# Attention: head pairs 3 to 5 prepared on the common plan, and two transposes moved to another PSUM ring

## The chip, the cores and the metric

The kernel runs on one core of a Trainium2 chip. The metric is device time in microseconds (us), lower is better; the time before is 658.43 us, the median of 3 runs.

## The reference

Attention with a cluster mask over 2 batches x 8 heads, 768 tokens, head size 64, then two dense blocks. The change touches the attention alone:

```python
q_assign = np.argmax(np.einsum('bhsd,hcd->bhsc', q_n, c_n), axis=-1)   # 16 clusters a head
k_assign = np.argmax(np.einsum('bhsd,hcd->bhsc', k_n, c_n), axis=-1)
mask = q_assign[:, :, :, None] == k_assign[:, :, None, :]
scores = np.where(mask, scale * np.matmul(q, k.transpose(0, 1, 3, 2)), -1000000000.0)
attn = np.exp(scores - np.max(scores, axis=-1, keepdims=True))
attn = attn / (np.sum(attn, axis=-1, keepdims=True) + 1e-09)
attn_out = np.matmul(attn, v)
# x = attn_out as 1536 x 512; then x @ w_in, leaky relu, @ w_out; then top-1 of 8 experts with a skip
```

## The kernel before

Two heads of one batch make a head pair, and there are 8 pairs, numbered 0 to 7. A pair takes 12 steps (six blocks of 128 queries for each of its two heads), so the loop at L689 runs 96 steps and some more to drain. One step puts on TensorE the scores of its block (`sps`, L371), the transposes of the probabilities of three steps before (`tps`, L428), and in every second step four matmul pairs with V (`avps`, L443). VectorE takes the row's maximum (`st`, L374), ACT the exponential with the row's sum (`pr`, L389) and the copies of the transposed probabilities to SBUF (`pt`, L435).

Each engine executes its instructions in the order in which the loop writes them. Nothing reorders them, so the order is set by hand.

While pair p runs, later pairs are prepared in the gaps. The function `plan(d)` lists, for one pair, at which step (counted from the start of the pair before; negative steps lie in the pair before that) each part is issued, and in which place of the step: "a0" after the scores, "d" and "pb" at its end. The parts, in order:

- `raw_pe` and `raw_act`, four times: q and k of the pair (tiles `natq`, `natk`) are transposed on TensorE into `rawps` (L179), and ACT copies that into `raw` (L191). After the fourth copy the load of the next pair's q and k is issued on SP's queue (L342, L99).
- `assign_pe`, `assign_act`, `argmax_pe`: products with the centroids (`asps`, L232), their copy (`sc`, L238), and their transpose (`scps`, L244).
- `argmax_0` to `argmax_3`: VectorE finds the best cluster and its one-hot `oh` (L269). One multiply in between, `eq` (L259), runs on GpSimd.
- `mask_pe` and `mask_dve`: the one-hot is transposed on TensorE (`ohps`, L292), and VectorE turns it into mask values `mk` (L298). `mask_dma` then copies these into the operands of the scores.
- `raw_split`, `exchange`: GpSimd splits `raw` into high and low parts (L208, L209), and DMAs copy them across partitions.

`PREPS` at L330 gives each pair its plan. Pairs 2, 3, 4 and 5 use `plan(5)`, `plan(4)`, `plan(3)` and `plan(2)`, pairs 6 and 7 use `plan(1)`. A larger d means later.

Of GpSimd's queue two more things matter. Every six steps it issues two loads `rb` (L414) of the reciprocals of the row sums. They wait until the row, transposed on TensorE (`rcps`, L406), copied by ACT (`rrow`, L408) and written to DRAM by SP (L704), has landed. And it multiplies the result `xr` by them and splits it (L457 to L467).

PSUM tiles come from rings by tag: "S" has two buffers of two banks for the scores, "T" two for the transposed probabilities, "A" one for `avps`, "M" one for nearly everything of the preparation and for `rcps`. A tile waits until the tile that had its buffer before is read. `raw`, `natq`, `natk` and `xr` have one buffer in SBUF each.

Of the kernel before, what the change touches and what calls it, by code (L numbers as in the profile page):

```python
# [11 lines left out]
BF16 = mybir.dt.bfloat16  # L12
# [13 lines left out]
def kernel(  # L26
# [20 lines left out]
    P = 128  # L47
# [30 lines left out]
    def ps_m(shape, name, dt=F32):  # L78
        return psum.tile(shape, dt, tag="M", name=name, bufs=1)
# [207 lines left out]
                                            op0=ALU.mult, op1=ALU.add)  # L287

    def mask_pe(p):
        ps = ps_m([P, 3, P], "ohps", BF16)  # L290
        for j in range(3):
            nc.tensor.transpose(ps[:, j, :], oh_t[p][:, j].rearrange("p g c -> p (g c)"), identb)  # L292
        ps_prep["mk"] = ps
# [19 lines left out]
    def plan(d):  # L313
        return [
            (d - 8, "pb", raw_pe, 0), (d - 7, "a0", raw_act, 0), (d - 7, "pb", raw_pe, 1),
            (d - 6, "a0", raw_act, 1), (d - 6, "pb", raw_pe, 2), (d - 5, "a0", raw_act, 2), (d - 5, "pb", raw_pe, 3),
            (d - 4, "a0", raw_act, 3), (d - 4, "pb", assign_pe, None),
            (d - 3, "a0", assign_act, None), (d - 3, "pb", argmax_pe, None),
            (d - 2, "d", argmax_0, None), (d - 2, "d", argmax_1, None), (d - 1, "d", argmax_2, None),
            (d, "d", argmax_3, None), (d + 1, "pb", mask_pe, None), (d + 2, "a0" if d == 2 else "d", mask_dve, None),  # L320
            (0, "a0", raw_split, 0), (1, "a0", raw_split, 1), (2, "a0", raw_split, 2), (3, "a0", raw_split, 3),
            (3, "d", exchange, 0), (5, "d", exchange, 1), (max(d + 2, 5), "d", mask_dma, None),
        ]

    PREP = plan(1)
    PREP0 = [(3, "a0", assign_act, None), (3, "pb", argmax_pe, None), (4, "d", argmax_0, None), (4, "d", argmax_1, None),
             (5, "d", argmax_2, None), (6, "d", argmax_3, None)]
    PREP1 = [(1, "pb", assign_pe, None), (2, "a0", assign_act, None), (2, "pb", argmax_pe, None), (3, "pb", argmax_0, None), (4, "pb", argmax_1, None), (5, "d", argmax_2, None), (6, "pb", argmax_3, None), (7, "pb", mask_pe, None), (8, "d", mask_dve, None),
             (8, "d", mask_dma, None)]
    PREPS = {0: PREP0, 1: PREP1, 2: plan(5), 3: plan(4), 4: plan(3), 5: plan(2)}  # L330

    def prep(p, r, slot):
        if p >= NP:
            return
        for rr, sl, f, arg in PREPS.get(p, PREP):
            if rr == r and sl == slot:
# [15 lines left out]
    NSTEP = B * NPAIR * 12  # L352
# [49 lines left out]
    rscr = nc.dram_tensor("recip_scratch", (NSTEP // 6, 6, P), F32, kind="Internal").ap()  # L402

    def recip_rows(g):
        ps = (ps_a if g == NSTEP // 6 - 1 else ps_m)([P, P], "rcps")
        nc.tensor.transpose(ps, rcs[g % 2], ident)  # L406
        row = att.tile([6, P], F32, tag="rrow", name="rrow", bufs=2)
        nc.scalar.activation(out=row, in_=ps[0:6, :], func=AF.Copy)  # L408
        rrow_t[g] = row
# [279 lines left out]
    for s in range(NSTEP + 12 + LAG):  # L689
        p, r = divmod(s, 12)  # L690
# [9 lines left out]
        if 0 < gf <= NSTEP // 6:  # L700
            if rf == 4:
                recip_rows(gf - 1)
            elif rf == 5:
                nc.sync.dma_start(rscr[gf - 1], rrow_t.pop(gf - 1))  # L704
        g, kt = divmod(s - 6 - LAG, 6)
# [876 lines left out]
```

## Time and profile before

| | |
|---|---|
| runs, median (lowest to highest) | 658.43 us (658.21 to 659.04) |
| profiled execution | 658.28 us, span 656.6 us |
| TensorE busy | 633.6 us, 96% |
| VectorE busy | 437.2 us, 67% |
| ACT busy | 420.8 us, 64% |
| GpSimd busy | 165.0 us, 25% |

The page calls the engines PE (TensorE), DVE (VectorE), ACT (ScalarE), POOL (GpSimd) and SP. The span runs from the first to the last instruction; the rest of the execution's time lies around it. Attention takes the first 256 us, the first dense block follows, then the experts. In the text "step" is a step of the attention loop, and step 0 of a pair is its first.

### The profile page before, as it was taken

The page shows a single profiled execution, that of the slowest core. Times are in us where ns is not written, and L with a number is a line of the kernel's source. Part 1 is how long each engine was busy: PE and PEld are TensorE (multiplying, and loading weights), DVE is VectorE, ACT ScalarE, POOL GpSimd, SP SyncE. Part 2 cuts the span into 40 slices and gives each one's busy share as a digit, 9 for nine tenths or more (in the row PEclk, how much of TensorE's full clock was granted, in tenths as well). Part 3 has the DMA queues.
Part 4 walks back from the last instruction along what each step waited for, and adds up shares of the span by engine and source line. Part 5 has one row for each costly group of instructions (what it writes and reads, how often), then busy time and mean ns, then how long its engine had stood idle before and what let it go on. Part 6 is the DMA issues. An engine that isn't in the chain of part 4 may idle for free.

```text
span 656.6 us, 10060 instructions
## 1 busy us (share of the span) xinstructions
PE 633.6 (96%) x3599; PEld 490.4 (75%) x3599; DVE 437.2 (67%) x767; ACT 420.8 (64%) x829; POOL 165.0 (25%) x215
## 2 busy tenths in 40 slices
PE   5999999989999999999999999999999999999995
PEld 3767766667767675788888888888888878688874
DVE  6756676676868663898765435645556548999971
ACT  5798887878888985655444444435654356688860
POOL 4234646463727333400000000000000025004211
PEclk9999999999999999999999999999999999999998
DMA  8765646577675518232104000007135337999930
GB/s 193 195 178 148 185 120 189 137 197 180 179 197 146 170 44 306 70 100 97 31 1 192 1 1 0 1 0 257 58 136 192 138 129 265 366 371 358 373 133 27
DMA packets 63636, 99.53 MB, mean 152 GB/s; under 512 B 27697, under 2 KB 31763, under 8 KB 63200
## 3 DMA queue, kind: packets, MB, share of 16 engines
q1 hardware_dynamic: 60304, 90.62, 44.1%
q0 software_dynamic: 3280, 8.24, 3.8%
q8 instruction: 29, 0.48, 0.3%
q14 instruction: 23, 0.19, 0.1%
HBM read 72.73 MB, written 12.70 MB: 130 GB/s over the span
## 4 chain that ended last, share of the span: by engine, by line
PE 83%; ACT 5%; DVE 5%; DMA 2%; issue 2%; POOL 2%; SPq 0%; POOLq 0%; DVEq 0%; ACTq 0%
PE acc L775 19%; PE ups L669 19%; PE sps L371 8%; PE avps L443 8%; PE hps L1273 7%; PE yps L1304 7%; PE tps L428 6%; ACT pr L389 3%; DVE st L374 1%; ACT pt L435 1%; PE hT L1285 1%; PE rawps L179 1%; PE acc L1165 1%; PE x2T L859 1%; PE asps L232 1%
## 5 line engine op out<-in xcount | busy, mean ns | idle before, releaser
L374 DVE TENSOR_REDUCE st<-sps 128x1 f32<-128x768 f32 x96 | 91.6, 955 | 59.8 <-PE sps L371 59.0
L435 ACT ACTIVATE pt<-tps 128x384 f32<-128x384 f32 x192 | 85.4, 510 | 20.0 <-PE tps L428 19.3
L389 ACT ACTIVATE pr<-sps,st 128x768 f32<-128x768 f32 x96 | 88.2, 919 | 14.3 <-DVE st L374 14.0
L428 PE MATMUL tps<-ident,pr 128*128 128x128 f32 x576 | 78.9, 273 | 0.5 <-ACT pt L435 0.5
L669 PE MATMUL ups<-xh,whii 128*128 128x512 f32 x192 | 74.8, 390 | 0.0
L669 PE MATMUL ups<-xh,wloi 128*128 128x512 f32 x192 | 74.7, 389 | 0.0
L669 PE MATMUL ups<-xl,whii 128*128 128x512 f32 x192 | 74.7, 389 | 0.0
L775 PE MATMUL acc<-whio,gh 128*128 128x512 f32 x183 | 73.1, 399 | 0.2 <-DVE g L759 0.2
L443 PE MATMUL avps<-pt,vnat 128*64 128x384 f32 x384 | 72.1, 498 | 0.0
L428 PEld LDWEIGHTS tps<-ident,pr 128*128 128x128 f32 x576 | 67.9, 140 | 5.5 <-ACT pt L435 1.6
L775 PE MATMUL acc<-whio,gl 128*128 128x512 f32 x183 | 71.4, 390 | 0.0
L775 PE MATMUL acc<-wloo,gh 128*128 128x512 f32 x183 | 71.3, 390 | 0.0
L760 ACT ACTIVATE gh<-g 128x512 fp32r<-128x512 f32 x48 | 30.4, 632 | 44.1 <-DVE g L759 44.1
L758 ACT ACTIVATE lk<-ups 128x512 f32<-128x512 f32 x48 | 28.5, 593 | 37.4 <-PE ups L669 30.9
L759 DVE TENSOR_TENSOR g<-ups,lk 128x512 f32<-128x512 f32 x48 | 33.1, 689 | 28.7 <-ACT lk L758 28.6
L762 DVE TENSOR_TENSOR gl<-g,gh 128x512 fp32r<-128x512 f32 x48 | 33.7, 702 | 25.1 <-ACT gh L760 25.1
L1013 POOL DMA_INDIRECT xe<-x_scratch,eix x1 | 1.2, 1169 | 190.0 <-DVE eix L1012 190.0
L646 DVE TENSOR_TENSOR wloi<-rawb,whii 128x512 fp32r<-128x512 f32 x36 | 24.7, 687 | 27.5 <-ACT whii L645 27.4
L443 PEld LDWEIGHTS avps<-pt,vnat 128*64 128x64 f32 x384 | 23.4, 136 | 25.3 <-issue 24.5
L669 PEld LDWEIGHTS ups<-xh,whii 128*128 128x128 f32 x192 | 36.0, 188 | 8.0 <-issue 0.6
L669 PEld LDWEIGHTS ups<-xh,wloi 128*128 128x128 f32 x192 | 36.1, 188 | 7.5
L669 PEld LDWEIGHTS ups<-xl,whii 128*128 128x128 f32 x192 | 36.0, 188 | 7.5
(303 smaller groups left out, 1353.4 us busy)
## 6 DMA issues: line engine op xcount, KB each, us to landing
rawb<-in_moe_w_dram SPq DMA_DIRECT2D x25, 1024.0 KB
rawa<-in_moe_w_dram SPq DMA_DIRECT2D x10, 1024.0 KB
stg<-in_moe_w_in_dram SPq DMA_DIRECT2D x16, 512.0 KB
stg<-in_moe_w_out_dram SPq DMA_DIRECT2D x16, 512.0 KB
UB<-UA SPq DMA_DIRECT2D x16, 192.0 KB
vnat<-in_v_dram SPq DMA_DIRECT2D x8, 384.0 KB
rb<-recip_scratch POOLq DMA_DIRECT2D x32, 96.0 KB, 2.8
w_f_scratch<-cvt SPq DMA_DIRECT2D x12, 256.0 KB
```

Of the source, the lines that this page charges most:

```text
L371: nc.tensor.matmul(ps[:, kh, 0:HS], lhsT=t[0:n, 0, qs], rhs=t[0:n, 1, kh * HS:(kh + 1) * HS], start=first, stop=not first)
L374: nc.vector.tensor_reduce(out=st[:, 0:1], in_=ps[:, :, 0:HS], axis=AX.XY, op=ALU.max, negate=True)
L389: nc.scalar.activation(out=pr, in_=ps[:, :, 0:HS], func=AF.Exp, bias=st[:, 0:1], accum_out=sm_t[g][:, 3 * h + j:3 * h + j + 1])
L428: nc.tensor.transpose(ps[:, t, :], pr[:, kh, t * P:(t + 1) * P], ident)
L435: nc.scalar.activation(out=pt[:, 3 * kh:3 * kh + 3, j, :], in_=t_t[s][kh], func=AF.Copy)
L443: nc.tensor.matmul(av_t[g][64 * h:64 * h + 64, :], lhsT=vnat[p][:, h, kt, :], rhs=pt_t[p, half, h][:, kt].rearrange("p j c -> p (j c)"), s ...
L669: nc.tensor.matmul(ps, lhsT=w[:, cc, :], rhs=x[:, blk, cc, :], start=(n == 0), stop=(n == 3 * KD - 1))
L759: nc.vector.tensor_tensor(out=g, in0=ps, in1=t, op=ALU.max)
L762: nc.vector.tensor_tensor(out=gl, in0=g, in1=_f(gh), op=ALU.subtract)
L775: nc.tensor.matmul(ps, lhsT=a[:, ts_], rhs=w, start=(fc == 0 and n == 0), stop=(fc == NFC - 1 and n == 2))
L1273: nc.tensor.matmul(ps, lhsT=x[:, c, :], rhs=w, start=(n == 0), stop=(n == len(mm) - 1))
L1304: nc.tensor.matmul(ps[:, cs], lhsT=x[:, f, :], rhs=w[:, cs], start=(h == 0 and f == 0 and n == 0), stop=(h == 1 and f == 3 and n == 2))
```

## The change

Pairs 3 to 5 get `plan(1)`, as pairs 6 and 7 have it; pair 2 keeps `plan(5)`. In `plan(d)` the place of `mask_dve` changes for d = 5 alone among the plans that are still used: it goes from step 7 to step 6, right behind `mask_pe`. Pair 2's transposed mask lies in the "T" ring and no longer in "M". The last `rcps` lies in "T" and no longer in "A".

```diff
     def mask_pe(p):
-        ps = ps_m([P, 3, P], "ohps", BF16)
+        ps = (ps_t if p == 2 else ps_m)([P, 3, P], "ohps", BF16)
...
-            (d, "d", argmax_3, None), (d + 1, "pb", mask_pe, None), (d + 2, "a0" if d == 2 else "d", mask_dve, None),
+            (d, "d", argmax_3, None), (d + 1, "pb", mask_pe, None), (d + (d < 5) + 1, "d" if d < 5 else "pb", mask_dve, None),
...
-    PREPS = {0: PREP0, 1: PREP1, 2: plan(5), 3: plan(4), 4: plan(3), 5: plan(2)}
+    PREPS = {0: PREP0, 1: PREP1, 2: plan(5)}
...
     def recip_rows(g):
-        ps = (ps_a if g == NSTEP // 6 - 1 else ps_m)([P, P], "rcps")
+        ps = (ps_t if g == NSTEP // 6 - 1 else ps_m)([P, P], "rcps")
```

On GpSimd, where pair 4 ends and pair 5 begins, the multiply `eq` (L259) of pair 5 stood behind the first split and the two `rb` loads. Before:

```order
L467 TENSOR_TENSOR xl<-xr,xh 128x256
L208 TENSOR_SCALAR UA<-raw 128x384
L209 TENSOR_TENSOR VA<-raw,UA 128x384
L414 DMA rb<-recip_scratch 64x384 x2
L259 TENSOR_TENSOR eq<-eq,cw 128x384
L208 TENSOR_SCALAR UA<-raw 128x384
```

And now:

```order
L467 TENSOR_TENSOR xl<-xr,xh 128x256
L259 TENSOR_TENSOR eq<-eq,cw 128x384
L208 TENSOR_SCALAR UA<-raw 128x384
L209 TENSOR_TENSOR VA<-raw,UA 128x384
L414 DMA rb<-recip_scratch 64x384 x2
L208 TENSOR_SCALAR UA<-raw 128x384
```

The multiply has moved ahead of both; it does the same for pairs 3 and 4.

On TensorE, in steps 6 to 8 of pair 1, behind the transposes of pair 2's mask (`ohps`), the `raw` transposes of pair 3 come in (one more group of them stands a step further up):

```order
 L292 MATMUL ohps<-identb,oh 128x128
-L371 MATMUL sps<-UB 128x384 x2
-L371 MATMUL sps<-VB 128x384 x2
-L428 MATMUL tps<-ident,pr 128x128 x6
+L179 MATMUL rawps<-ident,natq 128x128 x3
+L371 MATMUL sps<-UB 128x384 x2
+L371 MATMUL sps<-VB 128x384 x2
+L428 MATMUL tps<-ident,pr 128x128 x6
+L179 MATMUL rawps<-ident,natk 128x128 x3
```

Two groups of three transposes have come between the mask and the next steps' work.

On VectorE, in steps 6 and 7 of pair 1, the mask's reader (`mk`) of pair 2 stood behind the next maximum and the reciprocal. Before:

```order
L397 TENSOR_SCALAR sm<-sm 128x6
L374 TENSOR_REDUCE st<-sps 128x1
L400 RECIPROCAL rc_114<-sm 128x6
L298 TENSOR_SCALAR mk<-ohps,msc 128x384
L374 TENSOR_REDUCE st<-sps 128x1
```

And now:

```order
L397 TENSOR_SCALAR sm<-sm 128x6
L298 TENSOR_SCALAR mk<-ohps,msc 128x384
L374 TENSOR_REDUCE st<-sps 128x1
L400 RECIPROCAL rc_114<-sm 128x6
L374 TENSOR_REDUCE st<-sps 128x1
```

It stands one maximum earlier.

## Rows read from the trace of the kernel before

**Rows 1.** The page, parts 1 and 2: busy us; tenths in 40 slices.

```profile
PE 633.6 (96%) x3599; PEld 490.4 (75%) x3599; DVE 437.2 (67%) x767; ACT 420.8 (64%) x829; POOL 165.0 (25%) x215
...
PE   5999999989999999999999999999999999999995
```

**Rows 2.** Windows, pairs 1 to 5: stretch, width, busy us by engine, clock, DMA.

```profile
40.66:71.07 30.41, 29.99 (x203) 21.37 (x201) 20.49 (x34) 25.89 (x62) 16.14 (x21) 1.00 0.63 167
71.07:102.65 31.58, 30.64 (x207) 21.27 (x206) 21.17 (x34) 26.76 (x64) 15.67 (x21) 1.00 0.61 165
102.65:133.48 30.83, 29.90 (x203) 21.36 (x200) 20.52 (x33) 24.93 (x60) 17.16 (x21) 1.00 0.65 158
133.48:165.12 31.64, 29.45 (x199) 21.07 (x198) 21.65 (x34) 25.11 (x61) 14.80 (x19) 1.00 0.70 182
165.12:194.43 29.31, 29.31 (x200) 20.98 (x198) 22.31 (x34) 25.63 (x61) 16.43 (x21) 1.00 0.67 189
```

**Rows 3.** Waits of TensorE, 60 to 262 us: total, times, longest.

```profile
PE ohps L292 <- DVE oh L269: 1.7, 2, 1.1
PE rcps L406 <- DVE mk L298: 1.1, 1, 1.1
```

**Rows 4.** Timeline, pair 4: start, us, engine, what, [idle before, releaser].

```profile
137.89 1.11 POOL L414 DMA_DIRECT2D rb<-recip_scratch  x2 [5.19 <-DMA recip_scratch<-rrow]
...
139.01 1.02 POOL L259 TENSOR_TENSOR eq<-eq,cw 128x384 f32<-128x384 f32 x1
...
142.64 0.86 DVE L269 TENSOR_TENSOR oh<-eq,mx 128x384 bf16<-128x384 f32 x1
...
143.56 0.34 PE L292 MATMUL ohps<-identb,oh 128*128 128x128 bf16 x3 [1.12 <-DVE oh L269]
...
145.57 0.67 DVE L298 TENSOR_SCALAR mk<-ohps,msc 128x384 fp32r<-128x384 bf16 x1
...
146.38 0.30 PE L406 MATMUL rcps<-ident,rc 128*128 128x128 f32 x1 [1.07 <-DVE mk L298]
```

**Rows 5.** Timeline, pair 5, where pair 6 is prepared on plan(1).

```profile
166.85 1.01 POOL L259 TENSOR_TENSOR eq<-eq,cw 128x384 f32<-128x384 f32 x1 [4.10 <-DVE eq L256]
...
169.59 1.11 POOL L414 DMA_DIRECT2D rb<-recip_scratch  x2
...
172.46 0.34 PE L292 MATMUL ohps<-identb,oh 128*128 128x128 bf16 x3
...
178.91 1.00 POOL L209 TENSOR_TENSOR VB<-raw,UA 128x384 fp32r<-128x384 f32 x1
...
180.32 0.51 ACT L191 ACTIVATE raw<-rawps 128x384 f32<-128x384 f32 x1
```

**Rows 6.** Windows, steps 5 to 11 of pair 1 and of pair 5.

```profile
54.33:71.07 16.74, 16.41 (x113) 12.33 (x111) 11.99 (x20) 13.66 (x33) 7.30 (x10) 1.00 0.58 154
177.35:194.43 17.08, 17.08 (x121) 12.64 (x119) 11.33 (x17) 14.72 (x37) 6.37 (x10) 1.00 0.69 198
```

**Rows 7.** Timeline, pair 1, steps 6 and 7, around pair 2's mask.

```profile
58.68 0.34 PE L292 MATMUL ohps<-identb,oh 128*128 128x128 bf16 x3
...
59.61 0.82 PE L428 MATMUL tps<-ident,pr 128*128 128x128 f32 x6
59.94 0.17 DVE L397 TENSOR_SCALAR sm<-sm 128x6 f32<-128x6 f32 x1
```

**Rows 8.** Timeline, the end of attention.

```profile
254.55 0.49 ACT L451 ACTIVATE xr<-avps 128x384 f32<-128x384 f32 x1 [1.04 <-PE avps L443]
255.09 0.33 PE L406 MATMUL rcps<-ident,rc 128*128 128x128 f32 x1 [0.68 <-ACT xr L451]
...
260.20 0.49 ACT L451 ACTIVATE xr<-avps 128x384 f32<-128x384 f32 x1 [2.91 <-POOL xl L467]
```

**Rows 9.** DMA view, 42 to 48 us and 48 to 54 us: packets by size.

```profile
DMA packets 3330, 1.26 MB, mean 211 GB/s; under 512 B 3164, under 2 KB 3223, under 8 KB 3329
...
DMA packets 299, 0.89 MB, mean 148 GB/s; under 512 B 53, under 2 KB 53, under 8 KB 299
```

## The prediction

> **What bounds the kernel now.** I read the page first: TensorE is busy for 633.6 of 656.6 us, and in nine tenths and more of nearly every slice [rows 1]. The change touches the attention loop alone (8 head pairs of 12 steps, start to about 256 us) and adds and removes no instruction, so the question is where TensorE stands idle in that loop. The next view is one window per head pair, from the pair's first score matmul to the next pair's [rows 2]. Pair 5's window and pair 4's hold the same kinds and numbers of TensorE work (4 `raw` transposes of three, one `asps`, one `scps`, one `ohps`), yet pair 4 takes 31.64 us and pair 5 takes 29.31 us; the granted clock is 1.00 in both. Pairs 2 and 3 take 31.58 and 30.83 us. TensorE's idle time in the windows (width less busy) is 0.94, 0.93 and 2.19 us in pairs 2, 3 and 4, and nothing in pair 5.
>
> The list of waits says for what [rows 3]: the mask's transpose waits for VectorE's one-hot (1.7 us, twice), the reciprocals' transpose once for the mask's reader (1.1 us). The timeline of pair 4 shows the chain [rows 4]. GpSimd's queue is in order: `eq` of pair 5 stands behind the two `rb` loads, and these wait for the reciprocals' row to land in DRAM, until 137.89. So `eq` starts at 139.01, the one-hot ends at 143.50, TensorE has waited 1.12 us for it, and the mask's reader ends at 146.24, which holds the one "M" bank that the reciprocals' transpose needs: another 1.07 us. In pair 5 the pair being prepared is pair 6, which already has the plan that the change gives to pairs 3 to 5 [rows 5]: `eq` runs at 166.85, ahead of the `rb` loads at 169.59, and the mask's transpose at 172.46 waits for nothing.
>
> **The change part by part.** Each sum is made against the profiled execution (658.28 us, span 656.6); the median of the runs shown is 658.43, 0.15 us more, which I add at the end.
>
> *Pairs 3 to 5 prepared on plan(1).* Every instruction of their preparation moves 3, 2 and 1 steps earlier; the total of work stays. Pairs 2, 3 and 4 get exactly pair 5's content, so I price each by pair 5's window: 31.58 + 30.83 + 31.64 = 94.05 us becomes 3 x 29.31 = 87.93: **-6.12 us**. That includes the work that leaves pair 2 for pair 1 (pair 3's `asps` and `scps`).
>
> *Pair 1 gets fuller.* It keeps pair 2's last preparation and now holds all of pair 3's `raw`, `asps` and `scps`. From its sixth step on it has what pair 5 has there, plus pair 2's mask transposes. The two stretches take 16.74 us in pair 1 and 17.08 us in pair 5 [rows 6]; the three mask transposes are 0.34 us [rows 7]. So 17.42 - 16.74 = +0.68. ACT is late in this stretch: pair 2's `eq` still stands late on GpSimd, and the exponentials wait for VectorE. I allow between 0 and 0.4 us for `asps` waiting on ACT's last `raw` copy, and take **+0.8 us** in all.
>
> *Pair 3's load of q and k.* It is not moved, but its first reader goes from the ninth to the sixth step of pair 1, at 54.33. Between 42 and 48 us 3164 packets under 512 bytes ran, between 48 and 54 only 53 [rows 9]. The two loads make 2 x 1536 such packets (128 x 12 rows of 256 bytes each), so they had landed by about 48, 6 us ahead. Cost nothing; if the 6 us were gone, each us of lateness would be one us of TensorE.
> The Trainium skill (DMA: Bandwidth & Descriptors, Specifications) says that transfers under 512 B miss the line rate. That speaks against a reader that comes sooner; the rows show the load done in time all the same, and by them the sum stays.
>
> *Loads on SP's queue.* The q and k loads of pairs 4 to 6 go ahead of `vnat`, of a weight stage and of the reciprocals' row. This is the order that pair 4 already has for pair 7's load, and pair 5 behind it shows no wait for it. Between nothing and 0.4 us a pair; I take nothing.
>
> *Pair 2's mask in the "T" ring, its reader one step earlier.* The ring has two buffers, and the probabilities' second transpose of the next step now needs the mask's reader done. In pair 1 the mask's transposes run at 58.68 and that transpose follows from 59.61 on, while VectorE comes free for the reader at 60.11 (end of `sm`, 59.94 + 0.17) [rows 7]; with 0.67 us for the reader [rows 4] it ends at 60.78. Left alone that would hold TensorE for about 0.7 us, but two groups of three `raw` transposes stand ahead of it now; estimated at the mask group's 0.34 us each, they push TensorE back by 0.6 to 0.7. So 0.1 us, between 0 and 0.7; it lies in the +0.8.
>
> *Last reciprocals' transpose in the "T" ring.* It waits 0.68 us for ACT's `xr`, because both use the single "A" bank [rows 8]; the probabilities' last copies were done before `xr` began. The wait goes. What is late next: ACT's next `xr` at 260.20 waits for GpSimd, not for TensorE, so the chain behind it does not move fully along. Between 0 and 0.68; I take **-0.5 us**, nearer to the row.
>
> Sum: -6.12 + 0.8 - 0.5 = **-5.8 us**: 658.28 - 5.8 = 652.5, and with the 0.15 us 652.6 us. After attention TensorE's slices are full [rows 1], so what follows starts that much earlier and ends so.
>
> The Trainium skill (Perfetto Trace Analysis, Tensor Engine Instruction (MATMUL, LD_WEIGHTS)) warns that a matmul's reported end is computed, not observed. By this rule the idle time above misses part of the waiting, and start-to-start windows are the better measure; by idle time alone pairs 2 to 4 would give back 4.06 us and not 6.12. The rows bear it out for pair 4: it lost 2.33 us against pair 5 and shows 2.19 idle.
>
> **The rivals.**
> 1. *Only the visible idle returns.* TensorE's work is unchanged, so it can give back no more than it stood idle: 0.94 + 0.93 + 2.19 = 4.06 us, less the 0.4 us that I allowed for ACT in pair 1, and little at the end. For: the work of pair 3 that leaves pair 2 must be done in pair 1. Against: pair 2 loses 2.27 us to pair 5 with 0.94 idle, and its extra `asps` and `scps` need not be the whole rest. 658.43 - 3.7 = 654.7.
> 2. *The change does not do what it says.* Pairs 2 to 4 are slow because of what else runs there (weight stages, q and k loads), not because of the plan. Then the windows keep their widths, pair 1 pays 0.8 and the end returns 0.5: 658.7, no change. For: those loads are there. Against: the chain in rows 4 names GpSimd's order.
> 3. *Slower: the single `raw` buffer.* On plan(1) ACT's first `raw` copy of a pair overwrites what GpSimd's last split of the pair before still reads. In pair 5 that split ends at 179.91 and the copy starts at 180.32: 0.41 us of room [rows 5]. If GpSimd runs later than that in pairs 2 to 4 (its `rb` loads wait for the row's landing, and more q and k packets stand ahead of that row now), ACT blocks, and behind it the copies of the probabilities that TensorE waits for. Each us over 0.41 costs one us in three pairs. It eats the 5.8 us where GpSimd comes 0.41 + 5.8 / 3 = 2.3 us later than in pair 5; at 3 us it is 3 x 2.6 - 5.8 = +2.0: 660.4. Against: in pair 4, where the row lands just before 137.89, the `rb` loads go at 4.4 us into the pair, as in pair 5 (4.5).
>
> **How the numbers follow.** The forecast has 0.66, its own range 651.6 to 654.0 (all of -6.5 to -4.4). Rival 1 has 0.21, rival 2 has 0.07, rival 3 has 0.06. A measurement of this kernel tells 0.2% (1.3 us) from no change; so faster 0.87, same 0.07, slower 0.06. The range that holds 8 in 10 takes the forecast's and most of rival 1's: 651.5 to 656.2.
>
> **What would show it.** In the profile of the changed kernel the windows of pairs 2, 3 and 4 should be 29.0 to 29.6 us wide and pair 1 about 31.2; no wait of the mask's transpose for the one-hot longer than 0.2 us in pairs 2 to 4; `eq` of pairs 3 to 5 in the last step of the pair before, ahead of the `rb` loads; the last reciprocals' transpose without a wait for `xr`. A window of pair 1 above 32, or ACT's `raw` copy waiting for GpSimd, would make the forecast wrong, and so would windows of pairs 2 to 4 that stay above 30.5.

## The result and the profile after

The changed kernel takes 651.87 us, the median of 6 runs (650.17 to 654.0), against 658.4 us of the kernel before. The ratio is 0.9894 with an interval of 0.9873 to 0.9914, a gain of 5.7 to 8.4 us. The forecast of 652.6 us lies inside that interval, but the ratio's own value, 651.4 us (658.4 x 0.9894), lies 0.1 us under the low end of the range. The profiled execution took 651.22 us with a span of 649.3, 7.27 us less than the span before.

The page, parts 1 and 2, answers to [rows 1]:

```profile
PE 631.6 (97%) x3599; PEld 489.9 (75%) x3599; DVE 441.4 (68%) x767; ACT 420.8 (65%) x829; POOL 165.9 (26%) x215
...
PE   5999999999999999999999999999999999999994
```

TensorE does the same 3599 recorded matmuls, is booked as busy for 2.0 us less, and fills 97% of a shorter span. The windows of pairs 1 to 5 and, last, of pair 7 (columns as in [rows 2]; pair 7 has no successor, and its window runs to 0.52 us behind the start of the second group of probability transposes after the loop's last scores):

```profile
40.46:71.42 30.96, 30.87 (x213) 21.77 (x212) 20.71 (x34) 26.35 (x64) 13.96 (x19) 1.00 0.68 167
71.42:100.70 29.28, 29.28 (x199) 20.96 (x198) 22.57 (x34) 25.60 (x61) 16.46 (x21) 1.00 0.66 173
100.70:129.98 29.28, 29.28 (x199) 20.96 (x198) 22.54 (x34) 25.58 (x61) 16.47 (x21) 1.00 0.60 161
129.98:159.09 29.11, 29.11 (x199) 21.00 (x198) 22.50 (x34) 25.55 (x61) 16.13 (x21) 1.00 0.74 196
159.09:188.49 29.40, 29.26 (x199) 21.00 (x198) 21.60 (x34) 25.46 (x61) 16.52 (x21) 1.00 0.68 185
...
215.51:242.92 27.41, 27.16 (x175) 19.66 (x175) 16.91 (x25) 24.08 (x57) 8.72 (x14) 1.00 0.29 103
```

Pairs 2, 3 and 4 lost 2.30, 1.55 and 2.53 us against [rows 2], together 6.38, and TensorE no longer stands idle in them. Pair 1 grew by 0.55.

TensorE's waits in the same stretch as [rows 3], 60 to 262 us; this one row is the whole list:

```profile
PE tps L428 <- ACT pt L435: 0.5, 2, 0.3
```

The waits for the one-hot and for the mask's reader are gone; what is left stands at the drain of attention, where it was before too. [rows 3] shows two of the seven rows that this list had before. The others include 0.9 us of the scores for the exponential (three times) and 0.3 us of the mask's transpose for ACT's `rrow`. In pair 3 TensorE's waits were of these two kinds (0.48 and 0.34 us); none of the two for the one-hot lay there. The timeline of pair 4, rows that answer to [rows 4]:

```profile
131.71 1.01 POOL L259 TENSOR_TENSOR eq<-eq,cw 128x384 f32<-128x384 f32 x1 [4.10 <-DVE eq L256]
...
135.04 1.10 POOL L414 DMA_DIRECT2D rb<-recip_scratch  x2 [0.55 <-DMA recip_scratch<-rrow]
135.27 0.52 DVE L269 TENSOR_TENSOR oh<-eq,mx 128x384 bf16<-128x384 f32 x1
...
137.32 0.34 PE L292 MATMUL ohps<-identb,oh 128*128 128x128 bf16 x3
...
139.60 0.66 DVE L298 TENSOR_SCALAR mk<-ohps,msc 128x384 fp32r<-128x384 bf16 x1
...
140.35 0.30 PE L406 MATMUL rcps<-ident,rc 128*128 128x128 f32 x1
```

`eq` runs 3.3 us ahead of the `rb` loads, and the mask's transpose stands 1.53 us behind the end of the one-hot instead of waiting for it. The reciprocals' transpose follows the end of the mask's reader at 140.26 without a wait on TensorE.

The timeline of pair 5, rows that answer to [rows 5]:

```profile
165.43 1.12 POOL L414 DMA_DIRECT2D rb<-recip_scratch  x2 [1.82 <-DMA recip_scratch<-rrow]
...
173.91 1.31 POOL L209 TENSOR_TENSOR VB<-raw,UA 128x384 fp32r<-128x384 f32 x1
175.26 0.49 ACT L191 ACTIVATE raw<-rawps 128x384 f32<-128x384 f32 x1 [1.15 <-POOL VB L209]
```

Here the row landed later than before: the `rb` loads go 6.3 us into the pair, not 4.5, the last split ends late, and ACT's first `raw` copy waits 1.15 us for it. That is rival 3's mechanism, in one pair; the pair is 0.09 us longer for it.

The timeline of pair 1, steps 6 and 7, answers to [rows 7]:

```profile
58.81 0.34 PE L292 MATMUL ohps<-identb,oh 128*128 128x128 bf16 x3
58.99 0.50 PE L179 MATMUL rawps<-ident,natq 128*128 128x128 f32 x3
...
59.69 0.67 DVE L298 TENSOR_SCALAR mk<-ohps,msc 128x384 fp32r<-128x384 bf16 x1
60.02 0.95 PE L428 MATMUL tps<-ident,pr 128*128 128x128 f32 x6
```

The mask's reader ends at 60.36, while the six transposes of the probabilities run, and none of them waits in the list of waits. The end of attention answers to [rows 8]:

```profile
248.13 0.33 PE L406 MATMUL rcps<-ident,rc 128*128 128x128 f32 x1
248.34 0.49 ACT L451 ACTIVATE xr<-avps 128x384 f32<-128x384 f32 x1 [1.05 <-PE avps L443]
...
253.92 0.49 ACT L451 ACTIVATE xr<-avps 128x384 f32<-128x384 f32 x1 [3.38 <-POOL xl L467]
...
261.41 0.40 PE L775 MATMUL acc<-whio,gh 128*128 128x512 f32 x1
```

The last reciprocals' transpose now stands ahead of `xr`. The last row is the fourth matmul of the first dense block's output, without a wait. Before, it was the row

```profile
268.65 0.50 PE L775 MATMUL acc<-whio,gh 128*128 128x512 f32 x1 [0.16 <-DVE g L759]
```

From the last probability transposes' start to the reciprocals' transpose took 3.04 us before (252.05 to 255.09) and takes 2.30 now (245.83 to 248.13): 0.74 less. From the first to the fourth output matmul took 1.00 us before (267.65 to 268.65) and takes 0.69 now, and up to the tenth 0.41 us are gained. Nothing that follows in the dense blocks is spaced otherwise (0.07 us in 386).

### The profile page after: what moved, and what is told of

Read it like the earlier page. It is cut to its first block, busy times and chain, and to the rows that moved or that the text cites. A ratio compares the mean times of both kernels' runs of the same rounds, so it can differ in the third digit from the quotient of the medians.

```text
span 649.3 us, 10059 instructions
## 1 busy us (share of the span) xinstructions
PE 631.6 (97%) x3599; PEld 489.9 (75%) x3599; DVE 441.4 (68%) x767; ACT 420.8 (65%) x829; POOL 165.9 (26%) x215
## 4 chain that ended last, share of the span: by engine, by line
PE 92%; ACT 2%; POOL 2%; DVE 1%; DMA 1%; issue 1%; SPq 0%; POOLq 0%
PE ups L669 20%; PE acc L775 19%; PE sps L371 10%; PE avps L443 10%; PE tps L428 8%; PE hps L1273 7%; PE yps L1304 7%; PE rawps L179 1%; PE hT L1285 1%; PE acc L1165 1%; PE x2T L859 1%; ACT pr L389 1%; PE asps L232 1%; DMA recip_scratch<-rrow 1%; PE scps L244 1%; PE xT L1034 1%
```

## The experiments

Times in brackets after a median are the lowest and highest run; each ratio is to the kernel before, run on the same chip. The theory behind them: TensorE waited in pairs 2 to 4 because GpSimd's `eq` stood behind the `rb` loads ("G"). The rival: because VectorE's search fell in steps in which VectorE also converts weights ("V").

**The change again (after_again).** No edit.

> The changed kernel once more, unaltered, for a second profile and more rounds. By the theory that the gain lies in pairs 2 to 4, the windows of pairs 2, 3 and 4 are again 29.1 to 29.3 us, pair 1 about 31.0, and the time 650 to 654 us. If the gain outside pairs 1 to 4 (0.5 us in pair 7, 0.4 us in the first dense block) was chance of one execution, these two differ by a few tenths here.

651.85 us (651.7 to 652.4), ratio 0.9895, 0.9877 to 0.9914. Pairs 1 to 5 take 31.44, 29.27, 29.28, 28.99 and 29.95 us. So the gain repeats. Pair 7 takes 27.47 us and the end is as short as in the first profile, so neither was the chance of that one execution. Pair 5 again has ACT's `raw` copy behind GpSimd, 1.69 us this time, and TensorE waits 0.57 for it.

**The last transpose alone (rcps_only).** Kernel before, with

```diff
-        ps = (ps_a if g == NSTEP // 6 - 1 else ps_m)([P, P], "rcps")
+        ps = (ps_t if g == NSTEP // 6 - 1 else ps_m)([P, P], "rcps")
```

> The kernel before with the last reciprocals' transpose in T and nothing else. Theory: the wait of 0.68 us for xr goes and TensorE starts the first dense block 0.68 us earlier; of VectorE's later chain 0 to 0.4 us more. 657.3 to 657.8 us. Rival (the chain behind xr and GpSimd decides): the wait moves to the first dense block's second output product, and the time is within 0.2 us of before.

658.14 us (657.39 to 659.03), ratio 0.9985, 0.9973 to 0.9996. The median lies above the expected 657.3 to 657.8, on a chip where the kernel before took 658.81. In its profile the stretch at the last transposes is 0.74 us shorter than before and the one at the output matmuls, up to the tenth, 0.41; from the drain to the end of the program it gains 1.07 us. (The profiled span is as long as before, 656.6 us, because other stretches took longer in this execution, the start and pairs 1, 2 and 7.) So the trace gives this edit of one ring 1.07 us, the runs 0.3 to 1.8, and the wait for VectorE's `g` went with it: the second gain at the end belongs to this edit too. In the sixteen profiles of this case the reciprocals' transpose comes 2.30 us behind the last transposes wherever it lies in "T", and 3.04 to 3.05 wherever it lies in "A".

**The plans alone (plan1_mask_m).** The changed kernel with both rings put back: pair 2's mask in "M", the last `rcps` in "A".

> The change with pair 2's mask left in the M ring (its reader still at step 6) and the last reciprocals' transpose left in A. Theory: pairs 2 to 4 are 29.1 to 29.3 us as in the changed kernel; in pair 1 the second group of raw transposes waits for the mask's reader, 0.7 to 1.5 us, so pair 1 is 31.7 to 32.5; the wait of 0.7 us for xr at the end is back. In all 652.5 to 654.5 us. Rival (the T ring carries a good part of the gain): pairs 2 to 4 are above 30 us or pair 1 above 33, and the time is above 655 us.

654.56 us (654.26 to 655.65), ratio 0.994, 0.9925 to 0.9955. TensorE's waits from 50 to 270 us:

```profile
PE rawps L179 <- DVE mk L298: 1.3, 1, 1.3
PE rcps L406 <- ACT xr L451: 0.7, 1, 0.7
...
PE acc L775 <- DVE g L759: 0.3, 1, 0.3
```

Pair 1 takes 32.33 us, 0.9 to 1.4 more than with the mask in "T" (30.96 to 31.47 in five profiles): the next `raw` transposes want the "M" bank that the mask's reader holds. Pairs 2 to 4 keep 29.27, 29.28 and 29.00. So the plans bring the pairs' gain, and the rings keep pair 1 and the end from giving back some 2.7 us (of the medians).

**GpSimd's part taken out (eq_vector).** Kernel before, `eq` of pairs 3 to 5 on VectorE.

```diff
-        eng = nc.vector if p == 0 else nc.gpsimd
+        eng = nc.vector if p in (0, 3, 4, 5) else nc.gpsimd
```

> The kernel before with its plans of 5, 4, 3 and 2 steps, but the multiply eq of pairs 3, 4 and 5 on VectorE and no longer on GpSimd. Theory (eq behind the rb loads on GpSimd is the cause): the waits of the mask's transpose for the one-hot go, pairs 2 and 3 come to about 30.2 and 29.6 us (their own extra asps and scps stay), pair 4 to 29.3 to 30: some 3.5 to 4.5 us less than before, 654 to 655 us, without moving any preparation. Rival (the late plans themselves, by the M bank or by weight stages beside them): pairs 2 to 4 stay within 0.5 us of 31.6, 30.8 and 31.6, 658 us; VectorE's extra 0.56 us a pair costs nothing or a little.

659.06 us (658.28 to 661.74), ratio 1.001, 0.9998 to 1.0021: no gain, and G as the only cause falls. Its timeline in pair 3:

```profile
109.44 0.59 DVE L259 TENSOR_TENSOR eq<-eq,cw 128x384 f32<-128x384 f32 x1
109.71 1.19 POOL L209 TENSOR_TENSOR VB<-raw,UA 128x384 fp32r<-128x384 f32 x1
109.95 1.50 DVE L580 SCALAR_TENSOR_TENSOR cvt<-stg,cvt 128x512 uint32<-128x512 uint32 x1
...
111.37 0.95 DVE L374 TENSOR_REDUCE st<-sps 128x1 f32<-128x768 f32 x1
...
112.41 0.90 ACT L389 ACTIVATE pr<-sps,st 128x768 f32<-128x768 f32 x1 [2.74 <-DVE st L374]
...
113.45 0.44 PE L371 MATMUL sps<-UA 80*128 80x384 f32 x1 [1.65 <-ACT pr L389]
```

Here the wait has another name: the search and a weight conversion, this one drawn out beside GpSimd's split, stand ahead of the row's maximum in one step, so the exponential is 2.74 us late and TensorE's scores 1.65. In pair 4 the waits keep their names: 0.63 us for the one-hot (1.12 before) and the same 1.07 for the mask's reader.

**VectorE's part taken out (argmax_r3).** Kernel before with the search of pairs 3 to 5 moved to steps 3 to 6, where its first part meets no conversion; `eq` stays on GpSimd, the transposes of `raw` stay late, masks and the last `rcps` in "T".

```diff
+        v = 5 if d > 1 else 1
...
-            (d - 2, "d", argmax_0, None), (d - 2, "d", argmax_1, None), (d - 1, "d", argmax_2, None),
+            (v - 2, "d", argmax_0, None), (v - 2, "d", argmax_1, None), (v - 1, "d", argmax_2, None),
```

> The kernel before with the plans of 4, 3 and 2 steps for pairs 3, 4, 5, but VectorE's cluster search of these pairs at steps 3 to 6 as pair 2 has it (their masks in T, reader at step 6, the last reciprocals' transpose in T). Everything else of the preparation stays where it was. Steps 3, 7 and 11 hold no weight conversion on VectorE. Theory V (the search costs time where it shares a step with the conversions on VectorE): pairs 2, 3 and 4 fall to about 30.5, 30.0 and 29.7 us, 4 us less in all, and with 0.9 at the end 653.5 to 654.5 us. Theory G (eq has to stand ahead of the rb loads on GpSimd, which it does not here): pairs 2 to 4 stay above 30.8 on average and the time is 656.5 to 658 us.

658.49 us (657.68 to 659.48), ratio 0.9997, 0.9987 to 1.0006. V alone falls too. TensorE's waits from 60 to 160 us, and VectorE's wait for `eq` in pair 3:

```profile
PE tps L429 <- DVE mk L298: 1.9, 3, 0.8
PE ohps L292 <- ACT pt L436: 1.9, 2, 1.2
```

```profile
118.37 0.55 DVE L264 TENSOR_REDUCE mx<-eq 128x24 f32<-128x384 f32 x1 [3.19 <-POOL eq L259]
```

Pairs 2 to 4 take 31.70, 31.65 and 30.31 us, 0.39 less than before in all. At its new place `eq` still stands late on GpSimd, now behind the splits that the `rb` loads hold up, and VectorE waits 3.19 us for it in pair 3 and 2.70 in pair 4. Two parts of this edit have a price of their own: the end gains some 0.8 us from the last `rcps` in "T", and pair 1 is 0.94 us longer, 0.75 of it a wait for pair 2's mask in "T", which has no `raw` transposes behind it here.

**Both, by another way (r3_eq_vector).** The two edits above together; nothing is on `plan(1)`.

> Pairs 3 to 5 keep plan(4), plan(3), plan(2) for their transposes on TensorE, but VectorE's search stands at steps 3 to 6 (first part in step 3, which has no weight conversion) and the multiply eq is done by VectorE, so it passes GpSimd's rb loads altogether. The two halves of the theory are both met, by other means than plan(1). Theory 'both are needed and together they are enough': the waits of the mask's transpose in pairs 2 to 4 go, these pairs take 29.3 to 30.6 us, and the whole about 654 us (653 to 655.5). Rival 'the earlier raw and centroid work on TensorE and ACT is what counts': the pairs stay at 30.3 to 31.7 as with the search alone, and the whole at 658 to 659.

654.74 us (654.25 to 655.45), ratio 0.9938, 0.9917 to 0.996. Pairs 2 to 4 take 30.58, 30.51 and 29.94 us, and of their waits in [rows 3] nothing is left. The whole list from 60 to 165 us, of which the first row lies in pair 1:

```profile
PE tps L429 <- DVE mk L298: 0.8, 1, 0.8
PE rcps L407 <- DVE eq L256: 0.5, 2, 0.3
```

Each edit alone brought nothing, the two together 2.6 to 5.5 us, of which about 1 us is the last `rcps`, as in rcps_only. So two conditions go together: `eq` not late on GpSimd, and the first part of the search not beside a conversion. `plan(1)` meets both. One thing these runs do not separate: in eq_vector VectorE does the 0.59 us of `eq` itself, and no run has `eq` ahead of the `rb` loads on GpSimd with the search left where it was.

`plan(1)` is 2.9 us better still. In pairs 2 to 4 it gives back 6.38 us, these two edits 3.02. The three pairs hold 89.99 us of TensorE work here, as before, and 87.67 in the changed kernel; 1.27 us of that is one pair's `asps` and `scps`, which the change moves into pair 1. The other 2.1 us of the pairs' gain the two conditions do not explain, and no run takes them apart.

**The change without its order on GpSimd (eq_behind).** The changed kernel with `eq` of pairs 3 to 5 issued one step later, behind the `rb` loads (`argmax_1b` is that multiply alone).

```diff
-            (d - 2, "d", argmax_0, None), (d - 2, "d", argmax_1, None), (d - 1, "d", argmax_2, None),
+            (d - 2, "d", argmax_0, None), (d - 2, "d", argmax_1, None), (d - 1, "d", lambda q: argmax_1b(q) if 3 <= q <= 5 else None, None), (d - 1, "d", argmax_2, None),
```

> The changed kernel with one move: eq of pairs 3, 4 and 5 stands on GpSimd behind the rb loads (step 0) and no longer ahead of them; VectorE's compare stays in step 11. Theory G: VectorE stands in its queue until eq is done, some 2 us into each pair, so pairs 2, 3 and 4 become 1.5 to 3 us longer each, 31 to 32 us, and the time 656.5 to 660 us. Theory V: the search is still in a free step, the wait is covered by the two score buffers, pairs 2 to 4 stay below 29.8 us and the time is 652 to 653.5 us.

664.33 us (662.59 to 666.34), ratio 1.0077, 1.0057 to 1.0096. Pairs 2 to 4 take 32.65, 32.32 and 36.89 us. Waits of TensorE, 60 to 165 us, and then windows of 4 us in pair 4 (columns as in [rows 2]); L274 is the one-hot here:

```profile
PE ohps L297 <- DVE oh L274: 6.6, 3, 3.7
PE sps L376 <- ACT pr L394: 4.5, 3, 1.6
```

```profile
146.00:150.00 4.00, 1.37 (x11) 1.34 (x12) 4.00 (x8) 1.75 (x4) 3.27 (x4) 1.00 0.55 125
150.00:154.00 4.00, 2.68 (x11) 2.18 (x10) 3.23 (x5) 3.05 (x8) 1.51 (x2) 0.50 0.56 162
154.00:158.00 4.00, 4.00 (x18) 2.17 (x17) 1.38 (x2) 2.43 (x6) 2.66 (x4) 0.65 0.41 113
158.00:162.00 4.00, 4.00 (x29) 2.83 (x27) 3.61 (x6) 3.31 (x8) 0.19 (x1) 1.00 0.92 198
```

With the order on GpSimd undone the change costs 5 us instead of bringing 7, more than was expected. It is a harder case than the kernel before: there VectorE's next part of the search stands a step behind `eq`, here in the same step. In pair 4 the wait was 3.70 us long, and behind it the granted clock fell to 0.50, the lower level of 1.2 GHz, which makes this pair dearer than the other two; these had waits up to 1.63 us, and their clock stayed at 1.00.

**One pair alone (pair5_only).** Kernel before, pair 5 alone on `plan(1)`.

```diff
-    PREPS = {0: PREP0, 1: PREP1, 2: plan(5), 3: plan(4), 4: plan(3), 5: plan(2)}
+    PREPS = {0: PREP0, 1: PREP1, 2: plan(5), 3: plan(4), 4: plan(3)}
```

> The kernel before with pair 5 alone on plan(1); pairs 2 to 4 keep plan(5), plan(4), plan(3), the last reciprocals stay in A. Pair 5 is prepared while pair 4 runs. Theory 'each pair pays for its own successor's plan': pair 4 goes from 31.64 to 29.0 to 29.5 us, pair 3 (which takes over pair 5's earlier work) stays within 0.6 of 30.83, pairs 1 and 2 stay at 30.4 and 31.6; the whole 656 to 656.8. Rival 'the pairs disturb each other, the gain comes only when all are on the one plan': pair 4 stays above 30.3 or pair 3 loses what pair 4 gains; the whole 658 to 659. On pair 7, which went from 27.88 to 27.41 with the change: it goes with pair 5's plan if it is 27.3 to 27.6 here, and not if 27.8 or more.

657.69 us (656.57 to 659.53), ratio 0.9985, 0.9973 to 0.9997. The whole lies between the two forecasts. Pair 4 comes to 29.29 us, as expected, but pair 3 goes to 32.05, against the expectation. Pair 7 takes 27.96, so its gain does not come with pair 5's plan. The timeline of pair 3:

```profile
116.04 0.33 PE L292 MATMUL ohps<-identb,oh 128*128 128x128 bf16 x3 [0.34 <-ACT rrow L408]
...
118.36 0.67 DVE L298 TENSOR_SCALAR mk<-ohps,msc 128x384 fp32r<-128x384 bf16 x1
...
119.13 0.52 PE L179 MATMUL rawps<-ident,natq 128*128 128x128 f32 x3 [1.36 <-issue]
```

The profile names no releaser, but the transposes start 0.10 us behind the end of the mask's reader (119.03), and both tiles lie in the one "M" bank. Two plans side by side put pair 4's mask and pair 5's `raw` in the same steps; with one plan they lie apart. So here one pair's gain was taken back by its neighbour on another plan. The change avoids this at pair 2, which keeps `plan(5)`, by putting its mask into another ring.

**Rival 3 made to happen (gp_delay).** The changed kernel; GpSimd does the high part of the fourth split of pairs 3, 4 and 5 three, five and seven times over. There is one execution.

```diff
+        for _ in range(2 * (p - 2) + 1 if i == 3 and p in (3, 4, 5) else 1):
+            nc.gpsimd.tensor_scalar(out=hi, in0=raw[:, i, :], scalar1=1.0, scalar2=1.0, op0=ALU.mult, op1=ALU.mult)
```

> The changed kernel with GpSimd's last high-part split of pairs 3, 4 and 5 done 3, 5 and 7 times instead of once (the same values; about 1.0, 2.0 and 3.1 us more), to try the single raw buffer that rival 3 spoke of. By that rival, with about 0.4 us of room, pair 2 becomes 0.6 us, pair 3 1.6 us and pair 4 2.7 us longer than 29.3, 656 us in all, with ACT's raw copy waiting for GpSimd. If the probabilities' copies cover it, the pairs stay within 0.3 us of 29.3 up to 2 us of delay.

659.63 us. The last split ends 15.61, 17.69 and 21.04 us into pairs 2, 3 and 4 (14.37, 14.36 and 14.57 in the changed kernel). ACT's `raw` copies in these pairs:

```profile
87.25 0.49 ACT L191 ACTIVATE raw<-rawps 128x384 f32<-128x384 f32 x1 [0.33 <-POOL VB L210]
...
118.63 0.49 ACT L191 ACTIVATE raw<-rawps 128x384 f32<-128x384 f32 x1 [2.59 <-POOL VB L210]
...
152.95 0.49 ACT L191 ACTIVATE raw<-rawps 128x384 f32<-128x384 f32 x1 [6.05 <-POOL VB L210]
```

Pairs 2, 3 and 4 take 29.29, 30.97 and 35.87 us. A split 1.24 us later costs nothing, one 3.33 us later costs 1.69, and one 6.47 us later 6.76, the last with the granted clock at 0.59 and 0.56 in the two windows of 4 us from 150 to 158 us. TensorE waited 4.9 us until 153.49, so there the clock fell before the wait was over. The chain that rival 3 describes is real; its room is about 1.6 us (3.33 less 1.69) and not 0.41.

**Pair 2 on the common plan too (pair2_plan1, pair2_plan1_a).** The first drops `plan(5)` from `PREPS` and puts pair 1's mask, not pair 2's, in "T", with its reader at step 7 instead of 8. The second puts that mask back in "M" and spreads pair 2's `raw` transposes over "M" and "A":

```diff
-        ps = ((ps_t, ps_t, ps_m, ps_a)[i] if p == 0 else ((ps_t, ps_t, ps_a, ps_t)[i] if p == 1 else ps_m))([P, 3, P], "rawps")
+        ps = ((ps_t, ps_t, ps_m, ps_a)[i] if p == 0 else ((ps_t, ps_t, ps_a, ps_t)[i] if p == 1 else (ps_m, ps_a, ps_a, ps_m)[i] if p == 2 else ps_m))([P, 3, P], "rawps")
```

> The changed kernel with pair 2 on the common plan too: all pairs from 2 on. Its preparation then falls into steps 5 to 11 of pair 0; pair 1's mask goes through T with its reader at step 7. By both theories pair 1 becomes like pair 2, 29.3 us (1.7 to 2.1 less than now), and pair 0 gets three raw transposes, asps and scps more, 0.31 + 0.95 + 0.3 = 1.6 us of TensorE, part of it in its idle 1.3 us: 650.5 to 651.5 us. If ACT cannot take pair 0's copies in time, pair 0 grows by over 2 us and the time is 652 or more.

> The version with pair 2 on plan(1) too, with pair 2's raw transposes spread over the rings A and M (M, A, A, M) and pair 1's mask back in M. There pair 0 took 24.39 us against 23.17 with pair 2 on plan(5), and TensorE waited in it for ACT's raw copies (0.34 and 0.21) and for a probability copy (0.49). Theory 'the one bank M is what makes pair 0 wait': these waits go, pair 0 takes 23.2 to 23.7, the other pairs stay at 29.0 to 29.4, the whole 651.0 to 652.0, level with the changed kernel or 0.5 us faster. Rival 'ACT has no room in pair 0': the waits move to other tiles, pair 0 stays at 24.2 or more, the whole 652.5 to 653.5.

The first took 652.92 us (651.52 to 653.0), ratio 0.9908, 0.9892 to 0.9923: pair 1 fell to 29.37 as expected, but pair 0 rose to 24.39, and it is no better than the change. The second took 650.35 us (650.28 to 652.35), ratio 0.9873, 0.9853 to 0.9892. Its pair 0 takes 23.49, inside the expected 23.2 to 23.7, but not for the expected reason: 0.64 of the 0.90 lie in the very first step, where the first version waited 0.91 us for a DMA and the second did not. From step 6 on, pair 0 takes 13.81 and 13.54, so the rings were worth 0.3 us. In p2a_stg, below, which has the same rings, the wait in the first step is back, and pair 0 takes 24.46. TensorE's waits for ACT in pair 0 moved, as the rival had it. In the second version, 16 to 60 us:

```profile
PE rawps L179 <- ACT raw L191: 0.5, 1, 0.5
PE asps L232 <- ACT raw L191: 0.4, 1, 0.4
```

The two medians lie further apart than that, and the profiles don't show why. The second is the fastest version of the study by its median; its interval overlaps that of the change.

**Pair 7 (before_stg, after_stg, p2a_stg).** Pair 7 prepares nothing, and yet went from 27.88 to 27.41 us. In its first step ACT converts a weight stage. This conversion in the kernel before, and then in pair2_plan1_a:

```profile
223.50 0.89 ACT L573 ACTIVATE cvu<-stg 128x512 f32<-128x512 f32 x1 [0.53 <-DMA stg<-in_moe_w_in_dram]
```

```profile
218.91 0.66 ACT L573 ACTIVATE cvu<-stg 128x512 f32<-128x512 f32 x1 [1.66 <-DMA stg<-in_moe_w_in_dram]
```

The same load was late by 0.53 and 1.66 us, and not at all in the changed kernel. The three kernels are the one before, the changed one and pair2_plan1_a, each with that load issued half a step earlier:

```diff
+            elif r == 5 and m + 2 < NPC:
+                load_piece(*divmod(m + 2, 4))
             elif r == 6:
...
-                if m + 2 < NPC:
-                    load_piece(*divmod(m + 2, 4))
```

> The kernel before with each weight stage's load issued half a step earlier on SP (in the step's second conversion slot, right behind the last reader of its buffer, instead of in the next step). Theory 'chance of the landing': ACT's conversion in pair 7 waits for nothing, pair 7 takes 27.3 to 27.6 us instead of 27.88, the other pairs stay within 0.2, and the whole is 0.3 to 1.0 us faster than before, 657.4 to 658.1. Rival 'it is the change': pair 7 stays at 27.8 or more although the load lands earlier, since something else (ACT's queue) holds the conversion.

> The changed kernel with the weight stage's load half a step earlier. Theory 'chance': pair 7 stays at 27.4, the whole is at most 0.4 us faster than the changed kernel's 651.85, and the difference to before_stg is 6.2 to 6.9 us, what the pairs 1 to 4 and the end make without pair 7. Rival 'it is the change': the difference to before_stg is still 7.2 or more.

> Pair 2 on plan(1) too (raw transposes in M, A, A, M, pair 1's mask in M), with the earlier load. Its profile without that load had pair 7 at 28.76 us, 1.35 more than the changed kernel, and was 650.35 in the median all the same. Theory 'chance': pair 7 comes to 27.4, and the whole is 649.3 to 650.3, 1 to 2 us below after_stg on the same chip. Rival 'pair 0 gives it back': level with after_stg within 0.5 us.

They took 658.43 (657.72 to 660.1), 651.99 (650.41 to 652.44) and 650.84 us (649.64 to 651.47), with ratios 0.9991 (0.9977 to 1.0005), 0.9888 (0.986 to 0.9917) and 0.9872 (0.9843 to 0.99). Pair 7 takes 27.36, 27.35 and 27.41 us. The wait is gone in all three: pair 7's 0.47 us was the landing of one load. That the landing is chance and no part of the change is not shown. With the load where it was, the conversion waits 0.52 to 1.45 us in each of the six profiles of kernels that keep the late plans of pairs 3 and 4 (before, rcps_only, eq_vector, argmax_r3, r3_eq_vector, pair5_only), and at most 0.22 us in six of the seven with pairs 3 to 5 on `plan(1)`; pair2_plan1_a is the seventh. The times do not settle it: before_stg and after_stg are 6.4 us apart in the medians, inside the expected 6.2 to 6.9, but so are the two kernels without this edit (6.5), and the two profiled executions are 7.9 apart. before_stg missed its 657.4 to 658.1, and the earlier load itself gains nothing that the intervals show. p2a_stg missed its 649.3 to 650.3 and is 1.15 us under after_stg in the medians, with overlapping intervals: probably a gain, not shown.

## Why the prediction was nearly right, and which step failed

The terms as predicted, and in the two profiled executions, which differ by 7.27 us:

| term | predicted | measured |
|---|---|---|
| pairs 2 to 4 priced by pair 5 | -6.12 | -6.38 |
| pair 1 fuller | +0.8 | +0.55 |
| last reciprocals' transpose | -0.5 | -1.05 |
| pair 5 | 0 | +0.09 |
| pair 7 | 0 | -0.47 |
| pair 6, pair 0 and the start | 0 | -0.01 |
| sum | -5.8 | -7.27 |

**The step that failed** is the last reciprocals' transpose, "Between 0 and 0.68", taken at -0.5. The end of attention gave back 1.05 us in the change, 1.07 with this edit alone (rcps_only) and 1.02 between before_stg and after_stg: each is beyond the bound itself. The bound was the one idle time on the row. It missed, first, that start to start the place loses 0.74 and not 0.68. It missed, second, the steps after it: I argued that what stands behind `xr` waits for GpSimd and moves only in part, and did not follow the chain to the output matmuls, where TensorE's second wait, for `g`, cost 0.41 us and went too (of the two together 0.10 is lost again in between and behind). VectorE's three instructions ahead of that `g` (`gl`, `wloo`, `wloi`) took 1.23, 0.99 and 1.50 us before, each beside one of GpSimd's three on the last `xr`; they take 0.69, 1.51 and 0.98 now, because the first is under way before GpSimd starts. A mechanism that was right, with a term at half its size.

The sum also has no term for **pair 7**, which gave 0.47 us. The runs show that a late load made it, and leave open whether the change moves that load.

**Pairs 2 to 4** came out as priced, 0.26 us off over three windows, and each lies inside the forecast 29.0 to 29.6; rival 2 is out with them. Rival 1 is out too: pairs 1 to 4 together do the same work before and after, showed 4.48 us of idle time on TensorE and gave back 5.83. The 2.32 us by which pairs 2 to 4 beat their visible idle are not all waiting, since 1.27 of them went to pair 1 as work. Here the Trainium skill (Perfetto Trace Analysis, Tensor Engine Instruction (MATMUL, LD_WEIGHTS)) was right to warn that a matmul's end is computed: this trace agrees, with 1.4 us of busy time less in pairs 1 to 4 for the same work. The story behind the price was only half: I named GpSimd's order alone. eq_behind shows it is needed, eq_vector that taking `eq` off GpSimd is not enough, r3_eq_vector that it helps once the search has moved too. The price did not depend on that, since pair 5's window holds both.

**Pair 1**: +0.55 in this execution, +0.75 between before_stg and after_stg, and +1.03 in after_again (31.44 us), so +0.8 holds. Its stretch from step 5 on answers to [rows 6]:

```profile
54.13:71.42 17.29, 17.29 (x123) 12.73 (x122) 12.21 (x20) 14.13 (x35) 5.19 (x8) 1.00 0.66 154
```

I had put it at 17.42, and the allowance for ACT on top was not needed. The "T" ring cost nothing here. In three other executions it cost 0.22 us, the mask's transpose waiting for ACT to free the buffer, and 0.13 for the reader; without it pair 1 pays 0.9 to 1.4 (plan1_mask_m).

**The loads.** Pair 3's load of q and k was never waited for. SP's queue was not quite free: the reciprocals' row lands later in pair 5 (SP issues its write 1.71 us into the pair, where before it was issued 0.77 us ahead of it), and the pair pays 0.09 (after_again 0.6), where I had given 0 to 0.4.

**Rival 3** has its mechanism and not its size. "0.41 us of room" was read between the end of the split and the start of ACT's copy, but ACT's own queue has slack behind it: 1.24 us later cost nothing. And "ACT's `raw` copy waiting for GpSimd" was too strict as a sign against the forecast; it waited 1.15 us, and the pair lost 0.09. "Every instruction" of the preparation does not move: the splits stand at steps 0 to 3 in every plan, and that is why the copies come closer to them.

**The range.** Its low end let the gain go to 6.9 us (658.4 less 651.5), with nothing below for the end's missing half and for pair 7; these two were 1.0 us. It was also narrower than the prediction's own terms: windows of 29.0 us in pairs 2 to 4 give -7.05, and with +0.68 and -0.68 for the other two the time is 651.4. And the forecast's own range of 651.6 to 654.0 does not follow from "-6.5 to -4.4", which gives 651.9 at its low end.

## What to carry to other kernels

When a place in the trace already has the order that a change gives to others, start-to-start windows of the two price the change better than the sum of its waits. Do not let that price stand for the cause: here a wait that two in-order queues made did not go when one of them was mended, and in part only took a new name. And follow a removed wait to the next product that TensorE waits for before bounding it, since a bound of one idle row is no bound on the chain.

## What the runs showed of the hardware

A wait of 1.65 us on TensorE (eq_vector, pair 3) left its granted clock at 1.00 in the windows around it. Behind one of 3.70 us (eq_behind) it stood at 0.50 and 0.65 in the two windows of 4 us that follow, then at 1.00 again. In gp_delay the window from 150 us, in which most of a wait of 4.9 us lies, has 0.59, the next 0.56, and then 1.00. Such a wait is paid twice, for itself and at the lower clock.

One VectorE conversion of one shape (L580) took from 0.68 to 1.69 us within the changed kernel. The longest, with GpSimd beside it:

```profile
211.76 0.99 POOL L457 TENSOR_TENSOR xr<-xr,rb 128x384 f32<-128x384 f32 x1 [2.21 <-DMA rb<-recip_scratch]
211.77 1.69 DVE L580 SCALAR_TENSOR_TENSOR cvt<-stg,cvt 128x512 uint32<-128x512 uint32 x1
```

GpSimd's multiply starts 0.01 us ahead and ends at 212.75; with the conversion's usual 0.69 us from there the sum is 213.44, and it ended at 213.46. In eq_vector the same holds at the place where it hurt: GpSimd's split ran from 109.71 to 110.90, the conversion began at 109.95 and took 1.50 us. So some 0.8 us of that step's delay is this meeting (1.50 less 0.69).

The Trainium skill (SBUF — State Buffer, Who interferes with whom) says that a VectorE instruction with two inputs in SBUF contends with a GpSimd instruction that reads SBUF, and that the one that issues first holds the other off entirely. Both places agree with it, to 0.02 and 0.14 us.
